# A fused attention and feed-forward kernel: the second-layer block ahead of a new group's first layer, and another priority for the output copies

## Chip, cores and metric

The kernel runs on 1 core of one Trainium2 chip. The metric is the time of the kernel in device microseconds; the median of 3 runs stands for the kernel.

## What is computed

A long-short attention over B=4, H=8, S=768, D=64 gives the tokens of a two-layer feed-forward block with a rational activation. Cut to what matters:

```python
scores_l = scale * (q @ k.T)              # only where |i - j| < 16
scores_s = scale * (q @ k_blockmax.T) + log(32)   # 24 blocks of 32 keys
a = softmax(concat(scores_l, scores_s))
x = a @ concat(v, v_blockmean)            # -> x [3072 tokens, 512]

h = x @ w_in                              # 512 -> 2048
P = a0 + a1*h + a2*h*h + a3*h*h*h
Q = 1 + |b0|*|h| + |b1|*h*h
out = (P / (Q + 1e-6)) @ w_out            # 2048 -> 512
```

## The kernel before

The 3072 tokens are worked in six groups of 512 (`NG`), the 2048 inner columns in 16 chunks of 128 (`NFC`). A step is one chunk of one group, `step = 16 g + fc`; 96 steps make up the feed-forward part. Each step has these parts:

- `moe1` (L390): TensorE (PE) computes the chunk's h into one PSUM bank with twelve 512-column matmuls, eight with xh and four with xl, the upper and lower part of the group's x. `split` (L326) makes these parts at the first chunk of a group, four casts on ScalarE (ACT) and four subtractions on VectorE (DVE).
- `gelu` (L401): the activation. ACT makes the square of h (into tile sq or tq), |h| (ta) and an affine function of h (tu). DVE makes tq for the denominator; ACT takes its reciprocal through a logarithm and an exponential (`ta<-tq`, `ta<-ta`). DVE multiplies tu by h twice (`tu<-tu,h`, then `tu<-tu,cs,h`, the "second product", the last reader of the bank of h), then writes gh, tq and the last tu. GpSimd (POOL) writes gl from tu and ta. gh and gl are the upper and lower part of the activation. In steps without scores sq lies in a PSUM bank, otherwise the square is in tq in SBUF.
- `moe2` (L432): the second-layer block of the chunk three steps back (`LAG`), twelve matmuls into the four banks po_0 to po_3 (gh, gh, gl for each); `second_layer` (L451) takes it from a queue.
- `finish` (L441) at the last chunk of a group: ACT copies po_0 to po_3 into o_0 to o_3, and the DMA queue of SyncE (SP) writes them out. With the lag this falls into the new group's third step (fc = 2); the new group's first second-layer block, one step later, needs the copied banks.

PSUM holds four banks for po, two for h, and two for scores and sq. The attention of a half (64 tokens) is woven into the steps: every fourth step from step 14 on, two steps into each of groups 1 to 4 among them, PE multiplies probabilities and values (`av`, in one of the two banks of h) and makes new scores (`sc`), DVE masks the scores and takes the maxima (`ss`, `sm`), ACT takes the exponentials (`ss<-ss,sm`), and POOL normalizes them. ACT copies av to x (`x<-av`).

The tiles ta, tq and tu have two buffers, so ta of a chunk can be written only when gl of the chunk two steps back has been made; gh and gl have three.

The order of work has two regimes. In the first 14 steps (`NSTRICT`) each engine issues in the order of the text (`Kept`, L78 to L95). Afterwards PE alone is still kept in that order, while the Tile scheduler orders DVE, ACT, POOL and SP by a timeline simulation and by priorities: `tc.high_priority(offset=n)` puts what stands in it n places ahead. `split` has the offset 60 (L557), the activations -15 (L601), the attention 40 (L603). In the main loop (L547 to L625) `moe1` of a step comes first, then the activations, then the attention of the step, and `second_layer` (L623) comes last. At a border between groups PE therefore runs h of chunk 0 of the new group, then the block of chunk 13 of the old one, then h of chunk 1, then the block of chunk 14, and so on.

All engine calls pass the helper at L88, so that the profile gives this line for every instruction; tiles tell them apart.

Of the kernel before, what the change touches and what calls it, by code (L numbers as in the profile page):

```python
# [35 lines left out]
NG = NT // GT  # L36
# [24 lines left out]
def tile_kernel(ctx, tc, qw_in, kraw, kwin, vpad, vred, wio, a, b, cmask, cident, cavg, out):  # L61
# [109 lines left out]
    def value_average(av, vt, i):  # L171
        pe.matmul(av[:NK, :], avg[:, AVGW - NK - 4 * i:AVGW - 4 * i], vt[i], start=(i == 0), stop=(i == len(vt) - 1))
# [15 lines left out]
    def att_load(jj):  # L188
        bi, j = divmod(jj, NJ)
        nc.sync.dma_start(out=qw[jj % 2], in_=qw_in[bi, j])  # L190
        nc.sync.dma_start(out=kw[jj % 2][:, 0:NKC - 1], in_=kwin[bi, j])

    def key_blocks(jj):
        bi, j = divmod(jj, NJ)
        if j < 2 and bi > 0 or jj in (HPG, HPG + 1):
            dve.tensor_copy(kw[jj % 2][:, NKC - 1], ksum[bi])
# [51 lines left out]
    def load_v(jj):  # L248
        bi, j = divmod(jj, NJ)
        vt = vres[jj] if jj < HPG else vw[jj % 2]  # L250
        nc.sync.dma_start(out=vt[0:NKW, :], in_=vpad[bi, j * HQ:j * HQ + NKW, :])
        if j < 2 and bi == 1:
            nc.sync.dma_start(out=vt[NKW:NK, :], in_=vnext)
        elif j < 2 and bi > 1:
            nc.gpsimd.dma_start(
                out=vt[NKW:NK, :].rearrange("n (q d) -> n q d", q=4),
                in_=vsum[bi].rearrange("p c e -> p (c e)"))

    def turned(jj, early=False):
        pt = ps_h.tile([P, 512], F32, tag="h", name=f"pt{jj}") if early else ps_a.tile([P, 512], F32, tag="a", name=f"pt{jj}")  # L260
        for pr in range(NPAIR):
            pe.transpose(out=pt[:NK, pr * P:(pr + 1) * P], in_=att[jj][:, pr, :], identity=ident)
            if pr == NPAIR - 1:
                att[jj] = pt
            yield
# [60 lines left out]
    def split(g):  # L326
        if g == 0:
            return x32[0]
        xh = xp.tile([P, NCC, GT], F32R, tag="xh", name=f"xh{g}")
        xl = xp.tile([P, NCC, GT], F32R, tag="xl", name=f"xl{g}")  # L330
        for c in range(NCC):
            act.copy(xh[:, c], x32[g][:, c])
            dve.tensor_tensor(xl[:, c], x32[g][:, c], xh[:, c], op=ALU.subtract)
        return xh, xl
# [55 lines left out]
    def moe1(g, fc, xh, xl):  # L390
        h = ps_h.tile([P, GT], F32, tag="h", name=f"h{g}_{fc}")
        k = 0
        wt = weights(fc)
        for i, x in ((0, xh), (1, xh), (0, xl)):
            for cc in range(NCC):
                pe.matmul(h, wt[:, i, 0, cc * P:(cc + 1) * P], x[:, cc, :], start=(k == 0), stop=(k == 3 * NCC - 1))
                k += 1
        gh = gp.tile([P, GT], F32R, tag="gh", name=f"gh{g}_{fc}")
        gl = gp.tile([P, GT], F32R, tag="gl", name=f"gl{g}_{fc}")
        return gh, gl, gelu(h, gh, gl, g, fc)  # L400
# [31 lines left out]
    def moe2(fc, po, gh, gl, between):  # L432
        wt = weights(fc)
        for t in range(TPG):
            with tc.high_priority(offset=40):
                lead(between)
            ts_ = slice(t * P, (t + 1) * P)
            for i, (l, r) in enumerate(((gh, 0), (gh, 1), (gl, 0))):
                pe.matmul(po[t], l[:, ts_], wt[:, r, 1, :], start=(fc == 0 and i == 0),
                   stop=(fc == NFC - 1 and i == 2))  # L440

    def finish(g, po):
        for t in range(TPG):
            o = gp.tile([P, DM], F32, tag="o" if g < NG - 1 else "gl" if t % 2 else "gh", name=f"o{g}_{t}", bufs=4 if g < NG - 1 else 3)
            if g == NG - 1 and t % 2:
                dve.tensor_copy(o, po[t])
            else:
                act.copy(o, po[t])
            nc.sync.dma_start(out=out[g * GT + t * P:g * GT + (t + 1) * P, :], in_=o)

    def second_layer(step, queue, po, pt):  # L451
        if step >= LAG:
            g, fc, r = queue.pop(0)
            if fc == 0:
                po = [ps_o.tile([P, DM], F32, tag="o", name=f"po{g}_{t}") for t in range(TPG)]
            moe2(fc, po, *r, pt)
            if fc == NFC - 1:
                finish(g, po)
        return po

    cross = [tc.dram_tile([P, NKB, NPAIR, SQ], F32, name=f"cross{i}") for i in range(4)]
# [31 lines left out]
    def lead(chain, all_of=False):  # L493
        for _ in chain or ():
            if not all_of:
                return
# [5 lines left out]
    def whole(jj):  # L502
        yield from scores(jj)
        yield
        yield from values(jj)
# [42 lines left out]
    queue, po, x, gelus = [], None, None, {}  # L548
    for step in range(NG * NFC + LAG):
        g, fc = divmod(step, NFC)  # L550
        strictly = step < NSTRICT
        if step == NSTRICT:
            strict -= {dve, act, gps}
            for chain in [c for k, c in sorted(chains.items(), key=str)] + [gelus.pop(s) for s in sorted(gelus)]:
                lead(chain, True)
        if g < NG:
            if fc == 0:  # L557
                with tc.high_priority(offset=60):
                    x = split(g)
            gh, gl, gelus[step] = moe1(g, fc, *x)  # L560
            queue.append((g, fc, (gh, gl)))
        for what in STEP.split() if strictly else ():
            kind, n = what[0], int(what[1:] or 0)
            if kind == "g":
                lead(gelus.get(step - n))
            elif kind == "q":
                lead(prods.get(step - n))
            elif kind == "h":
                for jj in halves.get(step - n, ()):
                    lead(chains.setdefault(("h", jj), whole(jj)))  # L570
            elif kind == "k":
                for jj in halves.get(step - n, ()):
                    if jj > HPG + 1:
                        key_blocks(jj)
            elif kind == "l":
                for jj in halves.get(step - n, ()):
                    load_v(jj)
            elif kind == "a":
                for jj in halves.get(step - n, ()):
                    att_load(jj + 2)  # L580
            elif kind == "w" and fc + n < NFC and g == 0:
                lead(chains.setdefault(("w", fc + n), w_split(fc + n)))
            elif kind == "u":
                for f, *args in reduces.get(step, ()):
                    f(*args)
                for f, *args in loads.get(step, ()):
                    f(*args)
            elif kind == "P":
                pt = (z for jj in halves.get(step - n, ()) for z in turned(jj))
                po = second_layer(step, queue, po, pt)  # L590
                lead(pt, True)
            elif kind == "v" and step < LAG:
                if step == 0:
                    vf = ps_o.tile([P, DM], F32, tag="o", name="vf1")
                for i in range(2 * step, 2 * step + 2):
                    value_average(vf, fv1, i)
                if step == LAG - 1:
                    second_means(vf)
        if strictly:
            continue  # L600
        if step in gelus:  # L601
            with tc.high_priority(offset=-15):
                lead(gelus.pop(step), True)  # L603
        with tc.high_priority(offset=40):
            if step - 4 >= NFC - 2 and halves.get(step - 4):
                both_values(halves[step - 4][0])
            for jj in halves.get(step, ()):
                key_blocks(jj)
            if step in halves:
                chain = [scores(jj, sc=sc) for jj, sc in zip(halves[step], both_scores(halves[step][0]))]  # L610
            else:
                chain = ()
            for _ in range(5):
                for c in chain:
                    lead(c)
            for jj in halves.get(step - CROSS, ()):
                if jj >= 2 * HPG:
                    crossed(jj)
            for jj in halves.get(step, ()):
                load_v(jj)  # L620
                if jj + 2 < NHALF:
                    att_load(jj + 2)
        po = second_layer(step, queue, po, None)  # L623
        for f, *args in reduces.get(step, []) + loads.get(step, []):
            f(*args)  # L625

# [55 lines left out]
```

## Time and profile before

| | |
|---|---|
| median of 3 runs | 656.73 us (656.24, 659.31, 656.73) |
| the profiled execution: time | 654.91 us |
| the profiled execution: span | 653.1 us |
| granted TensorE clock, mean | 0.99 |
| DMA | 77.00 MB, mean 118 GB/s |

A row of a timeline or group of the profile names the start and duration in us, the engine, the line, the operation, output tile <- input tiles, shapes and the count; in brackets stand the idle time ahead of the row and what ended it. Rows of several instructions (x8) are back to back. The names of tiles leave out the chunk number there, so that the block is told by its place in time: the borders between groups lie near 155 to 167 us (group 0 to 1), 257 to 267, 357 to 367, 457 to 466 and 554 to 563 us. A matmul of a block counts at the rate of the block, since matmuls overlap in the rows.

### The profile page before, as it was taken

How to read it: one execution, taken by the hardware profiler on the slowest of the kernel's cores; microseconds unless marked ns; L12 is line 12 of the kernel's file. 1: busy time of each engine (PE TensorE's matmuls, PEld its weight loads, DVE VectorE, ACT ScalarE, POOL GpSimd, SP SyncE). 2: the span in 40 equal slices, each digit the busy share in tenths (PEclk: the TensorE clock that was granted, in tenths of full speed). 3: DMA queues.
4: the chain of work that ended last, by engine and by line, in shares of the span. 5: the costliest groups of instructions: out<-in, count | busy, mean ns of one | idle time of the engine just before them, and what ended most of it. 6: DMA issues, size and time to landing. Idle time of an engine off the chain costs nothing.

```text
span 653.1 us, 11832 instructions
## 1 busy us (share of the span) xinstructions
PE 627.3 (96%) x4068; PEld 499.4 (76%) x4068; DVE 577.2 (88%) x1148; ACT 460.4 (70%) x1036; POOL 258.9 (40%) x350
## 2 busy tenths in 40 slices
PE   8897989999999899999999999999999999999997
PEld 5664767776778688788888778888788888888886
DVE  5589999999989999988999989888888888988885
ACT  3979879977677667677677677577687576765652
POOL 1737567744343244343333333433433432222221
PEclk9989889999999999999999999999999999999999
DMA  9997643503354333242343253142152220010001
GB/s 323 333 321 240 239 166 112 182 25 114 107 171 131 102 122 120 84 166 95 112 127 113 73 193 86 63 128 66 64 174 83 64 86 2 13 52 1 0 2 64
DMA packets 51559, 77.00 MB, mean 118 GB/s; under 512 B 6068, under 2 KB 33076, under 8 KB 49580
## 3 DMA queue, kind: packets, MB, share of 16 engines
q1 hardware_dynamic: 50796, 75.80, 35.4%
q8 instruction: 32, 0.52, 0.3%
q10 hardware_dynamic: 576, 0.25, 0.1%
q0 software_dynamic: 128, 0.20, 0.1%
q14 instruction: 27, 0.22, 0.1%
HBM read 61.31 MB, written 14.73 MB: 116 GB/s over the span
## 4 chain that ended last, share of the span: by engine, by line
PE 60%; DVE 19%; ACT 9%; POOL 4%; issue 4%; DMA 2%; SPq 0%; DVEq 0%; POOLq 0%; ACTq 0%
PE po L88 27%; PE h L88 25%; DVE tu L88 6%; DVE tq L88 5%; PE sc L88 3%; POOL ss L88 3%; ACT ss L88 3%; DVE gh L88 3%; PE av L88 3%; ACT ta L88 2%; POOL gl L88 1%; DVE ss L88 1%; PE pt L88 1%; DMA kres<-in_kraw_dram 1%; PE vf L88 1%
## 5 line engine op out<-in xcount | busy, mean ns | idle before, releaser
L88 POOL TENSOR_TENSOR gl<-tu,ta 128x512 fp32r<-128x512 f32 x96 | 129.7, 1351 | 291.1 <-DVE tu L88 169.9
L88 POOL TENSOR_SCALAR ss<-ss,sm 128x120 f32<-128x120 f32 x192 | 98.6, 535 | 89.7 <-DVE sm L88 89.5
L88 PE MATMUL po<-wearly,gh 128*128 128x512 f32 x384 | 125.2, 408 | 1.4 <-ACT o L88 1.2
L88 ACT ACTIVATE ta<-tq,cs 128x512 f32<-128x512 f32 x96 | 69.5, 725 | 74.5 <-DVE tq L88 73.7
L88 PE MATMUL po<-w,gh 128*128 128x512 f32 x384 | 120.3, 394 | 0.0
L88 PE MATMUL h<-xh,wearly 128*128 128x512 f32 x384 | 98.1, 396 | 3.0 <-DVE tu L88 2.3
L88 PE MATMUL h<-xh,w 128*128 128x512 f32 x384 | 95.0, 389 | 0.0
L88 PEld LDWEIGHTS h<-xh,wearly 128*128 128x128 f32 x384 | 71.4, 188 | 23.5 <-DVE tu L88 4.5
L88 PEld LDWEIGHTS po<-wearly,gh 128*128 128x128 f32 x384 | 71.2, 193 | 19.4 <-ACT o L88 3.1
L88 ACT ACTIVATE ss<-ss,sm 128x120 f32<-128x120 f32 x192 | 73.4, 387 | 14.6 <-DVE sm L88 14.4
L88 PEld LDWEIGHTS h<-xh,w 128*128 128x128 f32 x384 | 72.0, 188 | 15.2 <-DVE tu L88 0.2
L88 PEld LDWEIGHTS po<-w,gh 128*128 128x128 f32 x384 | 70.8, 188 | 15.7 <-issue 1.3
L88 DVE SCALAR_TENSOR_TENSOR gh<-tu,cs,ta 128x512 fp32r<-128x512 f32 x96 | 73.8, 769 | 9.5 <-ACT ta L88 1.8
L88 ACT ACTIVATE ta<-h,cs 128x512 f32<-128x512 f32 x96 | 65.5, 682 | 19.1 <-POOL gl L88 18.9
L88 PE MATMUL po<-wearly,gl 128*128 128x512 f32 x192 | 76.3, 398 | 0.0
L88 DVE SCALAR_TENSOR_TENSOR tu<-tu,cs,tq 128x512 f32<-128x512 f32 x96 | 73.3, 763 | 2.5
L88 PE MATMUL po<-w,gl 128*128 128x512 f32 x192 | 74.9, 390 | 0.0
L88 ACT ACTIVATE tu<-h,cs 128x512 f32<-128x512 f32 x96 | 74.8, 779 | 0.0
L88 DVE SCALAR_TENSOR_TENSOR tu<-tu,cs,h 128x512 f32<-128x512 f32 x96 | 71.2, 742 | 2.2
L88 DVE SCALAR_TENSOR_TENSOR tq<-tq,gh 128x512 f32<-128x512 f32 x96 | 68.9, 718 | 2.8
L88 DVE TENSOR_TENSOR tu<-tu,h 128x512 f32<-128x512 f32 x96 | 64.9, 676 | 0.0
L88 DVE SCALAR_TENSOR_TENSOR tq<-tq,cs,ta 128x512 f32<-128x512 f32 x48 | 54.7, 1141 | 9.0 <-ACT ta L88 8.6
(72 smaller groups left out, 928.0 us busy)
## 6 DMA issues: line engine op xcount, KB each, us to landing
wr<-in_wio_dram SPq DMA_DIRECT2D x15, 1024.0 KB
cross<-tb SPq DMA_DIRECT2D x32, 256.0 KB
vw<-in_vpad_dram SPq DMA_DIRECT2D x42, 192.0 KB
kw<-in_kwin_dram SPq DMA_DIRECT2D x40, 192.0 KB
pts<-cross SPq DMA_DIRECT2D x96, 64.0 KB
out_dram<-o SPq DMA_DIRECT2D x24, 256.0 KB
qw<-in_qw_dram SPq DMA_DIRECT2D x40, 128.0 KB
kr<-in_kraw_dram SPq DMA_DIRECT2D x12, 384.0 KB
```

Of the source, the lines that this page charges most:

```text
L88: out = getattr(self.engine, name)(*args, **kw)
```

## The change

At the first chunk of groups 1 to 5 the second-layer block of the old group's chunk 13 is written ahead of `split` and `moe1` of the new group, instead of behind them at the end of the step. And `finish` gets `high_priority(offset=60)`.

```diff
--- before.py
+++ after.py
@@ -455,7 +455,8 @@
                 po = [ps_o.tile([P, DM], F32, tag="o", name=f"po{g}_{t}") for t in range(TPG)]
             moe2(fc, po, *r, pt)
             if fc == NFC - 1:
-                finish(g, po)
+                with tc.high_priority(offset=60):
+                    finish(g, po)
         return po
 
     cross = [tc.dram_tile([P, NKB, NPAIR, SQ], F32, name=f"cross{i}") for i in range(4)]
@@ -553,6 +554,9 @@
             strict -= {dve, act, gps}
             for chain in [c for k, c in sorted(chains.items(), key=str)] + [gelus.pop(s) for s in sorted(gelus)]:
                 lead(chain, True)
+        ahead = fc == 0 < g < NG
+        if ahead:
+            po = second_layer(step, queue, po, None)
         if g < NG:
             if fc == 0:
                 with tc.high_priority(offset=60):
@@ -620,7 +624,8 @@
                 load_v(jj)
                 if jj + 2 < NHALF:
                     att_load(jj + 2)
-        po = second_layer(step, queue, po, None)
+        if not ahead:
+            po = second_layer(step, queue, po, None)
         for f, *args in reduces.get(step, []) + loads.get(step, []):
             f(*args)
```

On PE, the only difference in the whole program is the place of h_0 at the five borders. The rows below are PE's at the border between group 1 and 2, before; h_0 and h_1 are first-layer blocks of the new group, the po block is chunk 13 of the old group.

```order
L88 MATMUL h_0_2943<-xh_2933,wearly 128x512 x8
L88 MATMUL h_0_2943<-xl_2934,wearly 128x512 x4
L88 MATMUL po_0_2108<-w_1505,gh_13_2720 128x512 x2
L88 MATMUL po_0_2108<-w_1505,gl_13_2721 128x512
L88 MATMUL po_1_2109<-w_1505,gh_13_2720 128x512 x2
L88 MATMUL po_1_2109<-w_1505,gl_13_2721 128x512
L88 MATMUL po_2_2110<-w_1505,gh_13_2720 128x512 x2
L88 MATMUL po_2_2110<-w_1505,gl_13_2721 128x512
L88 MATMUL po_3_2111<-w_1505,gh_13_2720 128x512 x2
L88 MATMUL po_3_2111<-w_1505,gl_13_2721 128x512
L88 MATMUL h_1_2986<-xh_2933,wearly 128x512 x8
L88 MATMUL h_1_2986<-xl_2934,wearly 128x512 x4
```

The same place after the change:

```order
L88 MATMUL po_0_2108<-w_1505,gh_13_2720 128x512 x2
L88 MATMUL po_0_2108<-w_1505,gl_13_2721 128x512
L88 MATMUL po_1_2109<-w_1505,gh_13_2720 128x512 x2
L88 MATMUL po_1_2109<-w_1505,gl_13_2721 128x512
L88 MATMUL po_2_2110<-w_1505,gh_13_2720 128x512 x2
L88 MATMUL po_2_2110<-w_1505,gl_13_2721 128x512
L88 MATMUL po_3_2111<-w_1505,gh_13_2720 128x512 x2
L88 MATMUL po_3_2111<-w_1505,gl_13_2721 128x512
L88 MATMUL h_0_2955<-xh_2945,wearly 128x512 x8
L88 MATMUL h_0_2955<-xl_2946,wearly 128x512 x4
L88 MATMUL h_1_2986<-xh_2945,wearly 128x512 x8
L88 MATMUL h_1_2986<-xl_2946,wearly 128x512 x4
```

h_0 now stands behind the twelve matmuls of the block and directly ahead of h_1; the blocks behind h_1 keep their places.

On DVE the scheduler takes the products of chunk 0 later. These rows stand directly behind gh_15, the upper part of the old group's last chunk, at the same border, before:

```order
L88 SCALAR_TENSOR_TENSOR tq_0_2959<-sq_0_2961,cs,ta_0_2958 128x512
L88 SCALAR_TENSOR_TENSOR tq_15_2890<-tq_15_2890,gh_15_2887 128x512
L88 TENSOR_TENSOR tu_0_2960<-tu_0_2960,h_0_2943 128x512
L88 SCALAR_TENSOR_TENSOR tu_15_2891<-tu_15_2891,cs,tq_15_2890 128x512
L88 SCALAR_TENSOR_TENSOR tu_0_2960<-tu_0_2960,cs,h_0_2943 128x512
L88 SCALAR_TENSOR_TENSOR gh_0_2956<-tu_0_2960,cs,ta_0_2958 128x512
L88 SCALAR_TENSOR_TENSOR tq_0_2959<-tq_0_2959,gh_0_2956 128x512
L88 SCALAR_TENSOR_TENSOR tu_0_2960<-tu_0_2960,cs,tq_0_2959 128x512
L88 SCALAR_TENSOR_TENSOR tq_1_3002<-sq_1_3004,cs,ta_1_3001 128x512
L88 TENSOR_TENSOR tu_1_3003<-tu_1_3003,h_1_2986 128x512
L88 SCALAR_TENSOR_TENSOR tu_1_3003<-tu_1_3003,cs,h_1_2986 128x512
L88 SCALAR_TENSOR_TENSOR gh_1_2999<-tu_1_3003,cs,ta_1_3001 128x512
```

And after:

```order
L88 SCALAR_TENSOR_TENSOR tq_15_2890<-tq_15_2890,gh_15_2887 128x512
L88 SCALAR_TENSOR_TENSOR tu_15_2891<-tu_15_2891,cs,tq_15_2890 128x512
L88 SCALAR_TENSOR_TENSOR tq_0_2971<-sq_0_2973,cs,ta_0_2970 128x512
L88 TENSOR_TENSOR tu_0_2972<-tu_0_2972,h_0_2955 128x512
L88 SCALAR_TENSOR_TENSOR tu_0_2972<-tu_0_2972,cs,h_0_2955 128x512
L88 SCALAR_TENSOR_TENSOR tq_1_3002<-sq_1_3004,cs,ta_1_3001 128x512
L88 TENSOR_TENSOR tu_1_3003<-tu_1_3003,h_1_2986 128x512
L88 SCALAR_TENSOR_TENSOR gh_0_2968<-tu_0_2972,cs,ta_0_2970 128x512
L88 SCALAR_TENSOR_TENSOR tu_1_3003<-tu_1_3003,cs,h_1_2986 128x512
L88 SCALAR_TENSOR_TENSOR tq_0_2971<-tq_0_2971,gh_0_2968 128x512
L88 SCALAR_TENSOR_TENSOR gh_1_2999<-tu_1_3003,cs,ta_1_3001 128x512
L88 SCALAR_TENSOR_TENSOR tu_0_2972<-tu_0_2972,cs,tq_0_2971 128x512
```

The rows of chunk 15 step ahead of those of chunk 0; the second product of chunk 1 (`tu_1_3003<-tu_1_3003,cs,h_1_2986`) comes as the ninth row instead of the eleventh, and the last tu of chunk 0 as the twelfth instead of the eighth. Ahead of gh_15 nothing moves at this border. Further on, in the step of the scores, the two products of chunk 2 stand behind the eight score instructions; before they stood ahead of them (at the border between group 2 and 3 one of the two did).

On ACT the copies move among the exponentials. These are its rows at the border between group 2 and 3, two steps into group 3, before; ss are the exponentials of the scores, o the output copies, ta_2 the activation of chunk 2:

```order
L88 COPY x_4162<-av_4163 128x4x128
L88 ACTIVATE ta_2_4147<-tq_2_4148,cs 128x512
L88 ACTIVATE ta_2_4147<-ta_2_4147 128x512
L88 ACTIVATE ss_4199,sm_4200<-ss_4199,sm_4200 128x120 x2
L88 COPY o_0_4251<-po_0_3210 128x512
L88 ACTIVATE ss_4199,sm_4200<-ss_4199,sm_4200 128x120 x2
L88 COPY o_1_4254<-po_1_3211 128x512
L88 ACTIVATE ss_4205,sm_4206<-ss_4205,sm_4206 128x120 x4
L88 COPY o_2_4257<-po_2_3212 128x512
L88 COPY o_3_4260<-po_3_3213 128x512
L88 ACTIVATE sm_4200<-sm_4200 128x4
```

And after:

```order
L88 COPY x_4162<-av_4163 128x4x128
L88 ACTIVATE ta_2_4147<-h_2_4132,cs 128x512
L88 ACTIVATE tu_2_4149<-h_2_4132,cs 128x512
L88 COPY o_0_4251<-po_0_3210 128x512
L88 ACTIVATE ta_2_4147<-tq_2_4148,cs 128x512
L88 ACTIVATE ss_4199,sm_4200<-ss_4199,sm_4200 128x120 x3
L88 COPY o_1_4254<-po_1_3211 128x512
L88 ACTIVATE ss_4199,sm_4200<-ss_4199,sm_4200 128x120
L88 ACTIVATE ss_4205,sm_4206<-ss_4205,sm_4206 128x120
L88 ACTIVATE ta_2_4147<-ta_2_4147 128x512
L88 COPY o_2_4257<-po_2_3212 128x512
L88 ACTIVATE ss_4205,sm_4206<-ss_4205,sm_4206 128x120 x2
```

The next row after this is `COPY o_3_4260<-po_3_3213 128x512`. The first copy moves ahead of ta_2's logarithm, the second exponential of ta_2 moves behind five of the eight ss, the last copy behind seven of them, and the copy of av moves ahead of ta_2's first row. At the borders between groups 1 and 2 and between 3 and 4 the copies keep their place behind ta_2's logarithm; there o_0 stands behind one ss, then come three ss, ta_2's exponential, o_1, three ss, o_2, one ss, and o_3 (before: ta_2's exponential, two ss, o_0, four ss, o_1, two ss, o_2 and o_3). On POOL and SP a few neighbours change places.

## The prediction

> **What bounds the kernel now.** I read the page first, then the waits of TensorE (PE), then the stretches around the five group borders in the timelines of PE, VectorE (DVE), ScalarE (ACT) and GpSimd (POOL). The page gives the busy time of each engine:
>
> ```profile
> PE 627.3 (96%) x4068; PEld 499.4 (76%) x4068; DVE 577.2 (88%) x1148; ACT 460.4 (70%) x1036; POOL 258.9 (40%) x350
> ```
>
> PE is busy for 627.3 of 653.1 us, so all its idle time together is 25.8 us, and no reordering can return more. The waits of PE say how much of that belongs to the borders (us in total, times, longest):
>
> ```profile
> PE av L88 <- DVE tu L88: 4.1, 4, 2.4
> ...
> PE h L88 <- DVE tu L88: 2.3, 4, 0.9
> PE h L88 <- DVE xl L88: 1.6, 2, 1.4
> ...
> PE po L88 <- ACT o L88: 1.2, 2, 1.0
> ```
>
> Steady PE work takes 2.72 us for each block of twelve 512-column matmuls, as the chain of waits shows:
>
> ```profile
> 288.31 2.72 PE po L88 x12
> ```
>
> I call the borders A (group 0 to 1), B, C, D, E, and a block by its chunk: h_0 is the new group's first, po_13 the old group's second-layer block that the change puts ahead of it.
>
> **The change, part one: po_13 ahead of h_0.** PE runs in the order of its list, and only h_0 moves in it; its twelve matmuls end behind po_13 instead of ahead of it, and h_1 follows. What matters is therefore what h_1 waits for. At B and C:
>
> ```profile
> 264.91 0.70 DVE L88 SCALAR_TENSOR_TENSOR tu<-tu,cs,h 128x512 f32<-128x512 f32 x1
> ```
>
> ```profile
> 265.67 2.11 PE L88 MATMUL h<-xh,wearly 128*128 128x512 f32 x8 [0.43 <-DVE tu L88]
> ```
>
> ```profile
> 364.20 2.12 PE L88 MATMUL h<-xh,wearly 128*128 128x512 f32 x8 [0.91 <-DVE tu L88]
> ```
>
> h_1 takes the PSUM bank of h_15, which the second product of chunk 15 frees: it ends at 264.91 + 0.70 = 265.61, and h_1 starts at 265.67. No DVE instruction moves ahead of that product, so h_1 starts then in both versions. Whatever h_0 waited for xl before reappears in the wait of h_1. **Gain at B and C from the order on PE: 0.** At D h_1 waits for nothing, so there is nothing to win. At E the question is whether h_2 now waits for the bank of h_0:
>
> ```profile
> 560.34 0.75 DVE L88 SCALAR_TENSOR_TENSOR tu<-tu,cs,h 128x512 f32<-128x512 f32 x1
> ```
>
> ```profile
> 564.77 1.98 PE L88 MATMUL h<-xh,wearly 128*128 128x512 f32 x8
> ```
>
> The bank is free at 561.09; h_0 comes one block later, 561.09 + 2.72 = 563.81, still 0.96 us ahead of h_2 at 564.77. **E: 0**, and up to +0.3 if the products of h_0, now behind two more of chunk 15, come over 0.96 us later still.
>
> A is the border that can lose. po_13 needs gl_13 at its third matmul:
>
> ```profile
> 158.53 1.27 POOL L88 TENSOR_TENSOR gl<-tu,ta 128x512 fp32r<-128x512 f32 x1
> ```
>
> ```profile
> 160.40 0.50 PE L88 MATMUL h<-xl,wearly 128*128 128x512 f32 x1 [1.44 <-DVE xl L88]
> ...
> 164.24 2.14 PE L88 MATMUL h<-xh,wearly 128*128 128x512 f32 x8 [0.55 <-DVE tu L88]
> ```
>
> gl_13 ends at 159.80. Ten of the twelve matmuls of po_13 follow (10 x 2.72 / 12 = 2.27, to 162.1), then h_0 to 164.8, where before h_1 started at 164.24: +0.6. The wait of h_0 for xl (1.44) disappears, and a wait of po_13 for gl_13 takes its place. I count this 0.6 at nothing, because a later wait of PE for DVE covers it:
>
> ```profile
> 224.53 1.15 PE L88 MATMUL av<-pts,vw 120*64 120x64 f32 x32 [2.40 <-DVE tu L88]
> ```
>
> PE stands 2.40 us there; DVE sets that time, so a PE that is 0.6 later waits 0.6 less. If DVE is itself late by the shift, A costs its +0.6.
>
> **Part two: what moves on DVE at B, C, D.** At the border's step 18 the attention's av matmuls use the PSUM bank of h_1 and wait for its second product:
>
> ```profile
> 274.65 1.15 PE L88 MATMUL av<-pts,vw 120*64 120x64 f32 x32 [0.52 <-DVE tu L88]
> ```
>
> ```profile
> 373.17 1.15 PE L88 MATMUL av<-pts,vw 120*64 120x64 f32 x32 [0.51 <-DVE tu L88]
> ```
>
> ```profile
> 471.98 1.15 PE L88 MATMUL av<-pts,vw 120*64 120x64 f32 x32 [0.69 <-DVE tu L88]
> ```
>
> In the new order that product is the ninth instruction behind gh_15, not the eleventh: two instructions of chunk 0 (about 0.7 us each by the rows below) step behind it, 1.4 us against waits of 0.5 to 0.7. These waits go. But that is no gain by itself: one step on, the new group's second layer reuses the po banks, and waits for the output copies of ACT. Whether PE arrives earlier there matters only if the copies do.
>
> **Part three: the copies, and what stands ahead of them.** Before, at B:
>
> ```profile
> 279.28 0.40 ACT L88 ACTIVATE ss<-ss,sm 128x120 f32<-128x120 f32 x1 [0.19 <-DVE sm L88]
> ...
> 280.05 0.57 ACT L88 COPY o<-po 128x512 f32<-128x512 f32 x1
> 280.52 0.40 ACT L88 ACTIVATE ss<-ss,sm 128x120 f32<-128x120 f32 x1
> ```
>
> ```profile
> 282.31 0.62 PE L88 MATMUL po<-wearly,gh 128*128 128x512 f32 x2
> ...
> 285.40 0.86 PE L88 MATMUL h<-xh,wearly 128*128 128x512 f32 x3
> ```
>
> ACT takes two ss exponentials in 280.05 - 279.28 = 0.77 (0.385 each) and 0.47 for a copy. PE loses 285.40 - 282.31 - 2.72 = 0.37 at B. At C and D:
>
> ```profile
> 379.21 0.38 ACT L88 ACTIVATE ss<-ss,sm 128x120 f32<-128x120 f32 x1
> ```
>
> ```profile
> 380.81 0.63 PE L88 MATMUL po<-wearly,gh 128*128 128x512 f32 x2
> ...
> 383.82 0.73 PE L88 MATMUL po<-wearly,gh 128*128 128x512 f32 x2 [1.04 <-ACT o L88]
> ...
> 385.32 1.98 PE L88 MATMUL h<-xh,wearly 128*128 128x512 f32 x8
> ```
>
> ```profile
> 476.60 0.40 ACT L88 ACTIVATE ss<-ss,sm 128x120 f32<-128x120 f32 x1 [0.19 <-DVE sm L88]
> ```
>
> ```profile
> 479.62 0.62 PE L88 MATMUL po<-wearly,gh 128*128 128x512 f32 x2
> ...
> 482.71 1.98 PE L88 MATMUL h<-xh,wearly 128*128 128x512 f32 x8
> ```
>
> The loss is 1.79 at C and 0.37 at D. The same distance holds at all three: from the first ss to the block h_4 behind the copies it is 6.12, 6.11 and 6.11 us. So the time of h_4 is the start of ss plus the length of ACT's list up to the copies, and I cost both.
>
> The list. Before, ta_2's second exponential stood ahead of the first ss; in the new order it stands among them, and at B and D all eight ss stand ahead of the last copy: 8 x 0.385 + 0.55 (ta_2, below) + 3 x 0.47 + 0.57 = 5.61, then one po block of three matmuls (0.68) and 0.05 for the hand-over: 6.34, **+0.23**. At C seven ss and o_1, o_2 are ahead of o_3: 4.76 + 0.73 = 5.5, **-0.6**.
>
> The start. The scores on DVE (ISA in the order's rows, CUSTOM_DVE in the trace) lose two products that stood ahead of them, but now wait for a chain that had slack: tu_0's last result, gl_0 on POOL, ta_2, tq_2. At B before:
>
> ```profile
> 269.82 1.22 DVE L88 SCALAR_TENSOR_TENSOR gh<-tu,cs,ta 128x512 fp32r<-128x512 f32 x1
> ...
> 271.80 0.75 DVE L88 SCALAR_TENSOR_TENSOR tu<-tu,cs,tq 128x512 f32<-128x512 f32 x1
> ...
> 276.91 0.75 DVE L88 SCALAR_TENSOR_TENSOR tq<-tq,cs,ta 128x512 f32<-128x512 f32 x1
> ...
> 278.96 0.27 DVE L88 CUSTOM_DVE_ANT_0 ss<-sc,mask 128x120 f32<-128x120 f32 x1
> ```
>
> ```profile
> 272.73 1.30 POOL L88 TENSOR_TENSOR gl<-tu,ta 128x512 fp32r<-128x512 f32 x1 [2.23 <-DVE tu L88]
> ```
>
> ```profile
> 278.45 0.63 ACT L88 ACTIVATE ta<-ta 128x512 f32<-128x512 f32 x1
> ```
>
> ```profile
> L88 ACT ACTIVATE ta<-tq,cs 128x512 f32<-128x512 f32 x96 | 69.5, 725 | 74.5 <-DVE tq L88 73.7
> ...
> L88 ACT ACTIVATE ta<-h,cs 128x512 f32<-128x512 f32 x96 | 65.5, 682 | 19.1 <-POOL gl L88 18.9
> ```
>
> tu_0's last result (271.80) goes from eighth to twelfth behind gh_15; four instructions of 0.72 make it 274.68 to 275.43. gl_0 then runs 275.6 to 276.9, ta_2 to 277.6, tq_2 to 278.35, and ta_2's logarithm to 279.07, where ss can start: -0.2 against 279.28. At D I take the same. At C tq_2 stands behind a reduction of another step, which covers this chain, and it was slow:
>
> ```profile
> 376.56 1.32 DVE L88 SCALAR_TENSOR_TENSOR tq<-tq,cs,ta 128x512 f32<-128x512 f32 x1
> ```
>
> It ended at 377.88, and ss started at 379.21 behind both halves of ta_2. The exponential now stands behind ss (-0.55), and with gl_0 out of the way tq_2 may take the 0.75 of B (-0.57): between -0.55 and -1.1, I take -0.9.
>
> One correction is open: DVE beside POOL. gh at 269.82 took 1.22 while gl ran; undisturbed the same instruction takes about 0.75. With gl_15 earlier, the instructions beside it read h or sq from PSUM, and I expect this 0.47 back; but gl_0 now falls beside two DVE instructions of chunk 1 whose inputs all lie in SBUF, which may hold it up by one of them, up to +0.7. Together -0.47 to +0.23; I take -0.1, near the middle, for B and D, and nothing at C, where the reduction covers it. By the Trainium skill, "SBUF — State Buffer", section "Who interferes with whom", a VectorE instruction with two SBUF inputs and a GpSimd one that reads SBUF exclude each other for a whole instruction; by that rule alone gl_0 is held up in full at all three borders, and the estimate would be 656.1 instead of 655.1. That gh took 1.22 agrees with it; gl_0 at 272.73 took an undisturbed 1.30 with DVE at work, which says no more than that DVE then read PSUM.
>
> **The sum.** A 0; B -0.2 - 0.1 + 0.23 = -0.1; C -0.9 - 0.6 = -1.5; D -0.1; E 0. Together -1.7, of the 653.1 us span. The profiled execution took 654.91, 1.8 more than its span; with the change 653.2. The runs of before have a median of 656.73, 1.8 above that execution, and the same difference gives **655.1 us** (656.73 - 1.7, rounded). Bounds: A 0 to +0.6; B and D from -1.0 (PE's own losses there, 0.5 to 0.7 at av and 0.37 at po, all gone) to +0.5; C from -2.3 (0.51 + 1.79 gone) to 0; E 0 to +0.3. All lows together -4.3, all highs +1.9.
>
> **The rivals.**
> 1. *The waits vanish whole (faster).* If ss starts early enough that all copies are done in time, av (0.52 + 0.51 + 0.69) and po (0.37 + 1.79 + 0.37) return 4.25 us: 652.5. If h_1's and h_0's waits went too (2.3 + 1.6 more), 648.6. For it: all these waits stand at borders. Against: DVE sets h_1's start, and ACT's list ahead of the copies gets no shorter at B and D. Chance 0.15, a third of it for the second kind.
> 2. *A new wait (slower).* The strict list on ACT makes the copies wait behind tq_2's chain. Such a wait of ACT for POOL is in the trace already:
>
> ```profile
> 270.53 0.69 ACT L88 ACTIVATE ta<-h,cs 128x512 f32<-128x512 f32 x1 [1.22 <-POOL gl L88]
> ```
>
> If the chain through gl_0 moves ss 1.22 later instead of earlier, B and D cost 1.22 + 0.23 each, C 1.22 - 0.6, A its 0.6: +4.1, 660.8. It decides as soon as ss starts more than 279.28 - 274.65 = 4.63 us behind the start of av. Against: the chain worked out above arrives 0.2 early. Chance 0.08.
> 3. *Nothing.* Copies and DVE cancel at C as well, and the time is that of before: 656.7. For it: the longest term, C, hangs on one reduction whose place is chance. Chance 0.25.
>
> My forecast, a gain at C alone, has 0.52.
>
> **How the numbers follow.** A measurement of this kernel can tell about 0.5%, 3.3 us, from no change. The range runs from 652.4 (the sum with all lows, and rival 1 of the first kind) to 658.6 (all highs); outside lie rival 2, the second kind of rival 1 and a little of the spread of the runs (656.24 to 659.31), 0.18 in all. Faster by more than 0.5% is below 653.4: rival 1 and a small part of the forecast's low side, 0.18. Slower is above 660.0: rival 2, 0.08. The rest, 0.74, is within 0.5%.
>
> **What would show it.** Right: at B and C h_1 still waits for DVE and starts as long after the old group's po_12 as before; av at B, C, D waits for nothing; at C the copies' wait shrinks by about 1.5 us, at B and D the distance from the first ss to h_4 grows to about 6.3; at A po_13 waits for gl_13 and the 2.40 wait shrinks by 0.6. Wrong: if h_1 comes earlier at B or C, if ss starts over 0.5 us from where I put it, or if h_2 waits for the bank of h_0.

## The result, and the profile after

| | before | with the change |
|---|---|---|
| median | 656.24 us (13 runs) | 661.33 us (13 runs) |
| ratio, with 95% interval | | 1.0073 (1.0051 to 1.0095) |
| profiled execution: time, span | 654.91, 653.1 us | 662.64, 660.9 us |
| granted clock of that execution | 0.990 | 0.977 |

The change costs 0.7%, about 5 us. The forecast was 655.1, a small gain. In the page's busy row PE and its weight loads grew most, by 5.3 and 6.7 us, though PE executes the same instructions. The row of the clock shows part of the reason. It gives the granted clock in 40 equal slices of the span, in tenths. The first and the sixth slice are lower than before, and the eleventh, 165 to 182 us, has an 8 (before, all slices from the seventh on were 9):

```profile
PE 632.6 (96%) x4068; PEld 506.1 (77%) x4068; DVE 579.3 (88%) x1148; ACT 459.3 (70%) x1036; POOL 257.4 (39%) x350
...
PEclk8989879999899999999999999999999999999999
```

The row of the clock before:

```profile
PEclk9989889999999999999999999999999999999999
```

The waits of PE after the change, in the same columns as before:

```profile
PE po L88 <- POOL gl L88: 4.1, 1, 4.1
PE po L88 <- ACT o L88: 3.4, 6, 0.8
...
PE av L88 <- DVE tu L88: 3.0, 2, 2.4
...
PE h L88 <- DVE tu L88: 1.0, 1, 1.0
PE av L88 <- DVE xl L88: 0.7, 1, 0.7
```

The waits of h for xl and most of those for tu are gone. Two have come: one of 4.1 us for gl, and six for the output copies in place of two.

To see where the time went, I took the start of each h block from the timelines of both traces and subtracted (after minus before, us; the step's number is 16 g + fc):

```
step 15   +3.39   (the start; the code is the same up to here)
step 18   +6.50   two blocks behind border A
step 26   +5.63
step 27   +7.18
step 34   +5.76   two blocks behind border B
step 36   +6.68   behind B's copies
step 47   +6.66
step 50   +6.65   two blocks behind border C
step 52   +5.62   behind C's copies
step 55   +6.22
step 66   +6.20   two blocks behind border D
step 68   +7.25   behind D's copies
step 95   +7.26
```

The first 3.39 us is no part of the change: the start scatters by that much between executions (the other traces below stand between -0.7 and +3.3 at step 15). What is left up to step 95 is 3.87. It falls at A (+2.24 by step 26), at the attention of step 26 (+1.55), at B ahead of the copies (-1.42, at h_1 and h_2), at the copies of B, C and D (+0.9, -1.0, +1.05), and ahead of step 55 (+0.6). The spans differ by 7.8 us: another half microsecond falls behind the last output copy; the end of the section on the prediction comes back to it.

**Border A.** The timelines of PE and POOL:

```profile
158.54 0.61 PE L88 MATMUL po<-w,gh 128*128 128x512 f32 x2
163.25 0.80 PE L88 MATMUL po<-w,gl 128*128 128x512 f32 x1 [4.09 <-POOL gl L88]
```

```profile
158.65 3.31 POOL L88 TENSOR_SCALAR ss<-ss,sm 128x120 f32<-128x120 f32 x4 [7.29 <-DVE sm L88]
161.93 1.26 POOL L88 TENSOR_TENSOR gl<-tu,ta 128x512 fp32r<-128x512 f32 x1
```

po_13 stops at its third matmul until gl_13 comes, behind four normalizations, at 163.19. Before, h_0 filled that time. And then the clock falls (the last columns are the granted clock, the DMA share and GB/s):

```profile
162.00:164.00 2.00, 0.76 (x2) 0.66 (x3) 2.00 (x3) 0.78 (x2) 2.00 (x3) 0.60 0.23 85
164.00:166.00 2.00, 2.00 (x7) 1.52 (x6) 1.71 (x3) 1.34 (x3) 1.49 (x4) 0.50 0.17 60
166.00:168.00 2.00, 2.00 (x6) 1.61 (x5) 2.00 (x5) 0.59 (x1) 0.00 (x0) 0.50 0.64 210
168.00:170.00 2.00, 2.00 (x7) 1.55 (x7) 1.97 (x3) 0.00 (x0) 1.16 (x1) 0.70 0.18 60
170.00:172.00 2.00, 2.00 (x10) 1.67 (x9) 1.78 (x2) 0.65 (x2) 0.50 (x2) 1.00 0.31 93
```

The clock is at half from about 162.4 to 169.2 us, and PE works in it from 163.25 on: the ten matmuls left of po_13 take 167.68 - 163.25 = 4.43 us, where the steady rate gives 2.27. The Trainium skill has this in "TensorE: Matmul & The Clock Gate", section "Part 1: The HAM clock gate (the "warmup" mystery)": an idle TensorE falls to half its clock, as a free-running window of about 3.4 us decides. The trace agrees in the 0.50, and in the window: by the clock column the half clock lasts (0.40 + 0.50 + 0.50 + 0.30) x 2 / 0.50 = 6.8 us, two times 3.4. Where it differs stands in the last section.

**Borders B and D.** The DVE rows of B ahead of the scores, with POOL's:

```profile
281.33 1.66 DVE L88 SCALAR_TENSOR_TENSOR tu<-tu,cs,tq 128x512 f32<-128x512 f32 x1
283.19 1.81 DVE L88 SCALAR_TENSOR_TENSOR tq<-tq,cs,ta 128x512 f32<-128x512 f32 x1 [0.21 <-ACT ta L88]
284.93 0.27 DVE L88 CUSTOM_DVE_ANT_0 ss<-sc,mask 128x120 f32<-128x120 f32 x1
```

```profile
280.86 1.57 POOL L88 TENSOR_TENSOR gl<-tu,ta 128x512 fp32r<-128x512 f32 x1 [5.90 <-DVE tu L88]
283.15 1.30 POOL L88 TENSOR_TENSOR gl<-tu,ta 128x512 fp32r<-128x512 f32 x1 [0.72 <-ACT ta L88]
```

The first DVE row is the last tu of chunk 1, the second tq of chunk 2; each takes about 0.75 us undisturbed, here 1.66 and 1.81, beside gl_0 and gl_1. At D they are 1.66 and 1.80. At B and D only the second of them reaches ss, because tq_2 has to wait for ta_2, and ta_2 for the end of gl_0:

```profile
282.47 0.69 ACT L88 ACTIVATE ta<-h,cs 128x512 f32<-128x512 f32 x1 [0.61 <-POOL gl L88]
```

The tu is done at 282.99, ta_2 only at 283.16. Then tq_2 takes 1.06 us more than 0.75: gl_1 started 0.04 us ahead of it. So ss comes late on ACT, and h_4 with it:

```profile
285.67 0.38 ACT L88 ACTIVATE ss<-ss,sm 128x120 f32<-128x120 f32 x1
```

```profile
288.80 0.73 PE L88 MATMUL po<-wearly,gh 128*128 128x512 f32 x2 [0.50 <-ACT o L88]
290.42 0.73 PE L88 MATMUL po<-wearly,gh 128*128 128x512 f32 x2 [0.66 <-ACT o L88]
292.08 1.08 PE L88 MATMUL h<-xh,wearly 128*128 128x512 f32 x4
```

From ss to h_4 it is 6.41 us (6.34 in the prediction). But ss is 6.39 us later than before while h of step 34 is 5.76 later: +0.63, where the prediction has -0.3. At D it is the same to 0.1 us:

```profile
483.55 0.38 ACT L88 ACTIVATE ss<-ss,sm 128x120 f32<-128x120 f32 x1
```

```profile
489.96 1.99 PE L88 MATMUL h<-xh,wearly 128*128 128x512 f32 x8
```

6.41 us again, and ss +0.75 against step 66. At C the list is shorter (5.56 us; 5.5 in the prediction), and the step gains:

```profile
385.38 0.38 ACT L88 ACTIVATE ss<-ss,sm 128x120 f32<-128x120 f32 x1
```

```profile
390.94 1.30 PE L88 MATMUL h<-xh,wearly 128*128 128x512 f32 x5
```

### The profile page after: what moved, and what is told of

It is laid out like the page before. It is cut to its first block, busy times and chain, and to the rows that moved or that the text cites. A ratio compares the mean times of both kernels' runs of the same rounds, so it can differ in the third digit from the quotient of the medians.

```text
span 660.9 us, 11836 instructions
## 1 busy us (share of the span) xinstructions
PE 632.6 (96%) x4068; PEld 506.1 (77%) x4068; DVE 579.3 (88%) x1148; ACT 459.3 (70%) x1036; POOL 257.4 (39%) x350
## 4 chain that ended last, share of the span: by engine, by line
PE 60%; DVE 19%; ACT 8%; DMA 5%; issue 4%; POOL 3%; DVEq 0%; SPq 0%; POOLq 0%; ACTq 0%
PE po L88 28%; PE h L88 26%; DVE tu L88 6%; DVE tq L88 5%; PE av L88 3%; DVE gh L88 3%; ACT ss L88 2%; PE sc L88 2%; ACT ta L88 2%; POOL ss L88 2%; DMA vr<-in_vpad_dram 2%; DMA kw<-in_kwin_dram 1%; POOL gl L88 1%; DMA vf<-in_vpad_dram 1%; DVE ss L88 1%
## 5 line engine op out<-in xcount | busy, mean ns | idle before, releaser
L88 DVE SCALAR_TENSOR_TENSOR tu<-tu,cs,tq 128x512 f32<-128x512 f32 x96 | 76.9, 801 | 2.4
```

The source lines that it names most:

```text
L88: out = getattr(self.engine, name)(*args, **kw)
```

## The experiments

The theories: (1) the stall at A, above all through the clock; (2) the copies at B and D, because DVE and POOL hold each other up; (3) the start alone. The ratio of each run is to the kernel before, with its 95% interval. The edits are shown against the kernel with the change, if nothing else is said; "..." marks what is left out. "Shift" is the start of an h block against the trace of before, as in the table above.

**The change without A.**

```diff
-        ahead = fc == 0 < g < NG
+        ahead = fc == 0 and 1 < g < NG
```

> The change at borders B to E alone; at A the order of before. Theory 1 (the cost is at A: the second-layer block of chunk 13 stands 4.1 us waiting for gl, and the granted clock then is 0.5 for about 7 us): no such wait, the clock at 155 to 170 us stays 1.00, and the time is that of before within +-0.3%, ratio 0.998 to 1.003. Theory 2 (the cost is at the copies of B and D, first ss late because DVE and POOL hold each other up): ratio 1.004 to 1.008, as for the whole change. Theory 3 (the cost is the start, ahead of step 14, where the profile of the change was already 3.4 us late): the ratio scatters with the start and says nothing of the borders.

Measured: 659.82 us, 1.0053 (1.0030 to 1.0077). The clock from 140 to 180 us stays 1.00, and the shift is +1.25 at step 15 and +1.22 at step 26: A costs nothing. Over B's copies (step 34 to 36) the shift goes from +1.36 to +2.28, over C's (50 to 52) from +2.29 to +1.23, over D's (66 to 68) from +1.79 to +2.84, as in the whole change. The ratio is where theory 2 has it: most of the cost is not at A.

**A alone, without the priority.**

```diff
-                with tc.high_priority(offset=60):
-                    finish(g, po)
+                finish(g, po)
...
-        ahead = fc == 0 < g < NG
+        ahead = fc == 0 and g == 1
```

> The reorder at border A alone, without the priority. Theory 1: the 4.1 us wait for gl and the dip of the clock are there, h two steps behind the border is about 3 us later than before, and 2 to 4 us of it are left at the end: ratio 1.003 to 1.006. Theory 2: ratio 0.999 to 1.002, since the later waits of PE for DVE (0.43 at B, 0.91 at C) take the delay back. Theory 3: as theory 2.

Measured: 657.85 us, 1.0029 (1.0004 to 1.0053). The wait for gl is 4.1 us again; the shift goes from +1.10 at step 15 to +3.69 at step 18 and +2.84 at step 26. So A costs as well, and the two parts, 0.29% and 0.53%, add up to the 0.73% of the change within their intervals. The trace shows too what becomes of A's delay. The wait of av for DVE, which the prediction had as its cover, has not shrunk:

```profile
227.35 1.97 PE L88 MATMUL av<-pts,vw 120*64 120x64 f32 x32 [2.40 <-DVE tu L88]
```

It was 2.40 before, too. DVE waited for the late h blocks too: between 160 and 180 us it was busy 19.71 us before and is busy 18.26 here (third figure behind the comma; the trace of before first, then this one).

```profile
160.00:180.00 20.00, 18.97 (x135) 14.85 (x136) 19.71 (x43) 13.51 (x28) 7.46 (x10) 1.00 0.36 113
```

```profile
160.00:180.00 20.00, 19.04 (x128) 15.42 (x129) 18.26 (x27) 10.61 (x18) 7.50 (x10) 0.86 0.22 71
```

At B, where this kernel has the old order, the shift falls from +4.29 at step 31 to +2.86 at step 34. In the run without A, with the new order there, it falls by the same 1.43, from +2.79 to +1.36. There a late PE gets time back, in either order, because DVE frees the bank of h_15 at its own time. What is paid back so is the clock dip at step 26, not A's delay: the unchanged wait of 2.40 us says that up to there DVE is as late as PE. In all five traces of this document with such a dip the shift falls by 1.43 from step 31 to 34; in the four others that have a wait at step 26, it moves by 0.06 at most.

**The priority alone.** Against the kernel before.

```diff
             if fc == NFC - 1:
-                finish(g, po)
+                with tc.high_priority(offset=60):
+                    finish(g, po)
```

> The priority of the output copies alone, no reorder. All theories: PE, DVE and ACT have the rows of before, so ratio 0.999 to 1.001; what it scatters is the spread of the start. If the priority itself were the cause: 1.004 or more.

Measured: 656.70 us, 1.0009 (0.9987 to 1.0032): nothing. The shift is +2.70 at step 15 and +2.64 at step 95, so the start is all that differs.

**The reorder alone, without the priority.**

```diff
-                with tc.high_priority(offset=60):
-                    finish(g, po)
+                finish(g, po)
```

> The reorder at all five borders without the priority. Theory 1 and 2: ratio 1.005 to 1.009, as the whole change or a little worse, since the last copies stand behind all eight ss. If the priority were the cause: 0.998 to 1.002.

Measured: 660.48 us, 1.0063 (1.0040 to 1.0086). The reorder is the cause. At D the shift rises more than in the whole change, from +2.95 at step 67 to +6.59 at step 69, since all eight ss now stand ahead of o_2; the times of the two kernels don't tell them apart.

**A alone, with twelve matmuls without use ahead of po_13.** They go into the bank of h_0, which h_0 then overwrites; the priority of `split` goes from 60 to 72 with them. The edits of the run with A alone are left out here.

```diff
+        filled = None
         if ahead:
+            filled = ps_h.tile([P, GT], F32, tag="h", name=f"h{g}_{fc}")
+            for k in range(12):
+                pe.matmul(filled, weights(fc)[:, 0, 0, :P], weights(fc)[:, 1, 0, :], start=True, stop=True)
             po = second_layer(step, queue, po, None)
...
-                with tc.high_priority(offset=60):
+                with tc.high_priority(offset=60 if filled is None else 72):
                     x = split(g)
-            gh, gl, gelus[step] = moe1(g, fc, *x)
+            gh, gl, gelus[step] = moe1(g, fc, *x, filled)
```

> The reorder at A alone, with twelve matmuls without use (2.72 us, into the bank of h_0, which h_0 then overwrites) ahead of the second-layer block, so that TensorE stands 4.1 - 2.7 = 1.4 us instead of 4.1. Up to there nothing else moves; behind step 18 some DVE and ACT rows of groups 1 and 2 do. Theory 1a (the length of the stall brings the clock down, and that is most of the loss at A): the granted clock between 160 and 172 us stays 1.00, h of step 18 starts +0.3 to +0.8 us later than before instead of +2.5 (relative to step 15). Rival 1b (the loss is the wait for gl itself, whatever PE does meanwhile): +2.3 or more, as without the filling. Time: 1a ratio 0.999 to 1.003; 1b 1.002 to 1.005.

Measured, the place that the run was made for:

```profile
161.50 0.50 PE L88 MATMUL po<-w,gl 128*128 128x512 f32 x1 [1.40 <-POOL gl L88]
```

```profile
160.00:164.00 4.00, 2.60 (x12) 2.06 (x12) 3.47 (x5) 1.89 (x3) 3.74 (x7) 1.00 0.18 66
164.00:168.00 4.00, 4.00 (x20) 3.30 (x18) 3.97 (x7) 1.40 (x3) 0.91 (x1) 1.00 0.40 131
```

The clock stays at 1.00, and the shift goes from +1.61 at step 15 to +2.07 at step 18: +0.46, against +2.59 without the filling, though gl comes no earlier and PE does 2.7 us more. So the clock is 2.1 of the 2.6 us. The total, 659.10 us, 1.0046 (1.0022 to 1.0070), misses the expectation: the filling makes the scheduler place DVE and ACT rows of step 18 and later differently, and the shift jumps from +2.36 to +5.28 at step 20, part of which comes back at step 27 (+1.91). The total therefore says nothing about A.

**A alone, with gl_13 on DVE.** The edits of the run with A alone are left out again.

```diff
-        gps.tensor_tensor(gl, tu, ta, op=ALU.mult)
+        (dve if g * NFC + fc == NSTRICT - 1 else gps).tensor_tensor(gl, tu, ta, op=ALU.mult)
```

> The reorder at A alone, with gl of chunk 13 made by DVE instead of POOL, which has four normalizations ahead of it. The wait of the second-layer block for gl gets shorter by about 2 us, to about 2; DVE's later rows come 0.7 us later. Theory 1a: no dip or a short one, h of step 18 +0.5 to +1.0 relative to step 15, ratio 0.999 to 1.003. Rival 1b: +0.5 to +1.0 as well; what tells them apart is whether the clock falls. If neither holds and POOL is not the cause: +2.3 or more.

Measured: 656.09 us, 1.0009 (0.9987 to 1.0031).

```profile
157.07 0.50 PE L88 MATMUL po<-w,gl 128*128 128x512 f32 x1 [2.04 <-DVE gl L88]
```

```profile
156.00:158.00 2.00, 0.93 (x3) 0.79 (x4) 1.79 (x4) 2.00 (x5) 2.00 (x3) 0.87 0.00 0
158.00:160.00 2.00, 2.00 (x6) 1.51 (x6) 1.69 (x3) 0.42 (x1) 2.00 (x5) 0.50 0.06 23
160.00:162.00 2.00, 2.00 (x9) 1.60 (x8) 2.00 (x4) 0.90 (x2) 0.67 (x2) 0.78 0.29 109
```

The clock fell here too, but after a wait of 2.04 us and for half the time, some 3.4 us, and the shift is -0.73 at step 15 and -0.70 at step 18. h_1 follows h_0 at once and comes 0.28 us late (-0.45 at step 17); the 0.55 us that it waited for DVE before took up the rest, and ahead of h_2, where PE stood before as well, nearly all of the 0.28 is made good. So it is POOL's place for gl_13 that made A cost anything.

**B to E, with gl_0 of groups 2 to 4 on DVE.**

```diff
-        ahead = fc == 0 < g < NG
+        ahead = fc == 0 and 1 < g < NG
...
-        gps.tensor_tensor(gl, tu, ta, op=ALU.mult)
+        (dve if fc == 0 and 1 < g < NG - 1 else gps).tensor_tensor(gl, tu, ta, op=ALU.mult)
```

> The change at B to E (as in the run without A), with gl of chunk 0 of groups 2 to 4 made by DVE instead of POOL. Theory 2a (DVE and POOL hold each other up: tu_1 took 1.66 and tq_2 1.81 instead of 0.75 beside gl_0 and gl_1): these two take 0.75 to 1.2, ss starts 0.5 to 1.3 us earlier at B and D, and B and D together cost 0.5 us or less instead of 2; ratio 1.001 to 1.004 against 1.0053 without. Rival 2b (the later place of chunk 0 in DVE's order is the cost, not the beside): DVE is 0.7 us later by the added instruction, ss starts as late as or later than in the change, and the ratio is 1.005 to 1.007.

Measured: 655.47 us, 0.9978 (0.9957 to 1.0000), against 1.0053 with gl_0 on POOL. The same DVE rows of B:

```profile
277.26 0.69 DVE L88 TENSOR_TENSOR gl<-tu,ta 128x512 fp32r<-128x512 f32 x1
277.86 0.75 DVE L88 SCALAR_TENSOR_TENSOR tu<-tu,cs,tq 128x512 f32<-128x512 f32 x1
278.70 0.75 DVE L88 SCALAR_TENSOR_TENSOR tq<-tq,cs,ta 128x512 f32<-128x512 f32 x1
```

```profile
280.12 0.38 ACT L88 ACTIVATE ss<-ss,sm 128x120 f32<-128x120 f32 x1
```

DVE has an instruction more and is done sooner: 1.66 and 1.81 are now 0.75 and 0.75. ss is 0.84 later than before where h of step 34 is 1.50 later: -0.66 instead of +0.63. Of these 1.29 us, 0.24 come from the earlier end of gl_0, which lets ta_2 and tq_2 start earlier, and 1.05 from tq_2 itself. Now tq_2 starts ahead of gl_1, by 0.08 us, and it is gl_1 that is held up:

```profile
278.78 1.83 POOL L88 TENSOR_TENSOR gl<-tu,ta 128x512 fp32r<-128x512 f32 x1 [7.78 <-ACT ta L88]
```

The kernel before had the same pair in the same order: tq_2 at 276.91 took 0.75, and gl_1 1.66:

```profile
277.16 1.66 POOL L88 TENSOR_TENSOR gl<-tu,ta 128x512 fp32r<-128x512 f32 x1 [3.14 <-DVE tu L88]
```

From step 31 to 37 the shift falls by 0.45, from 63 to 69 by 0.57, where in the run without A it rose by 1.03 in the latter. Theory 2a holds, rival 2b falls.

**gl_0 on DVE alone, in the order of before.** The same edit to gl, in the kernel before.

> The kernel before, its order and priorities unchanged, with gl of chunk 0 of groups 2 to 4 made by DVE. Theory 2a (POOL and DVE hold each other up only in the new order, where gl_0 stands beside DVE rows that read SBUF alone): nothing to win here, since gl_0 ran beside rows that read PSUM; DVE has one instruction of 0.7 us more at three borders: ratio 0.999 to 1.003. Rival 2c (gl_0 on DVE is a gain in itself, and the reorder had no part in the 0.9978 of the run with both): 0.996 to 0.999.

Measured: 657.21 us, 1.0012 (0.9986 to 1.0037). No gain shows: gl_0 on POOL costs time only where the reorder puts it. This trace has its clock dip at step 26, which stands in the order of before: a wait of 2.44 us, the clock at 0.50 from about 228 to 234, and the shift goes from +3.32 to +6.20 at step 27. So the +1.55 that the trace of the change shows there isn't the change's either; it comes and goes with the execution.

**The whole change, gl_0 and gl_13 on DVE.** Both edits to gl together.

> The whole change, with gl of chunk 0 of groups 2 to 4 and gl of chunk 13 at border A made by DVE: both suspected costs taken out. Theories 1 and 2a together: A costs nothing at the steps behind it (the wait for gl is about 2 us, hidden by DVE's own delay of h_1), B to D gain about 1.4 us as before: ratio 0.996 to 1.000. If a third cost is at work in the change: 1.002 or more.

Measured: 655.34 us, 0.9988 (0.9970 to 1.0006). The shift is +1.33 at step 15, +1.38 at step 18, +1.33 at step 31, +0.90 at step 37, +0.58 at step 55, +0.02 at step 95: A costs nothing, and B, C and D gain 0.44, 0.32 and 0.57. With the two costs out, no loss of the change is left. That it or the run before it beats the kernel before by more than a measurement tells isn't shown: both intervals reach 1.0.

## Why the prediction was wrong, point by point

- **h_1 starts with DVE at B and C, so the order on PE wins nothing there.** Right. Where PE came late it lost its wait at B and got 1.43 us back, with the old order as with the new. At E nothing moved, as predicted.
- **A: "+0.6 ... I count this 0.6 at nothing".** Wrong twice. With the clock at 1.00 the term was good (+0.46 with the filling). But the wait it rests on is 4.09 us long, and the trace shows PE at half its clock for some 6 us behind it: +2.6 to +3.1 at step 18. The working had the granted clock at full throughout. And the cover failed: the 2.40 us wait for DVE stayed at 2.44, because h_0 and h_1 came late to DVE as well. A wait of PE for DVE covers a late PE only if DVE isn't late by the same cause; the condition stood in the prediction and was taken the wrong way.
- **av's waits at B, C, D go.** Right, except that this is no gain by itself, as the prediction says.
- **The length of ACT's list: 6.34 and 5.5.** Right: 6.41, 5.56 and 6.41.
- **The start of ss at B and D: "-0.47 to +0.23; I take -0.1".** This step failed. DVE beside POOL cost not one collision but two: gl_0 held the last tu of chunk 1 (+0.9), and gl_1, which follows that tu at once, held tq_2 (+1.06). The working saw only gl_0. Up to tq_2 its chain was good: less the shift of 5.76, gl_0 ended at 276.67 at B (276.9 in the working) and ta_2 at 277.40 (277.6), because the held tu was done by then. The step that failed is "tq_2 to 278.35": tq_2 took 1.81 instead of 0.75 and ended at 279.24. So ss is 0.93 (B) and 1.05 us (D) later than forecast, and each costs about 1 us instead of winning 0.1. The rule of the Trainium skill cited there, "SBUF — State Buffer", section "Who interferes with whom", is what the traces show: DVE's 1.66 and 1.81 beside POOL's gl, 0.75 without. Its estimate in the prediction, 656.1, counted one collision as well.
- **C: -1.5.** Half right: -1.0 behind the copies. The list gained its 0.6, but ss came 0.5 us earlier, not 0.9: the held tu took 1.66 us here too, with DVE busy from it through the reduction and tq_2 to the scores, so the reduction did not cover it as the working had it:

```profile
381.05 1.66 DVE L88 SCALAR_TENSOR_TENSOR tu<-tu,cs,tq 128x512 f32<-128x512 f32 x1
382.63 1.21 DVE L88 TENSOR_REDUCE vs<-vr 96x32 f32<-96x1024 f32 x1
383.76 0.96 DVE L88 SCALAR_TENSOR_TENSOR tq<-tq,cs,ta 128x512 f32<-128x512 f32 x1
384.64 0.27 DVE L88 CUSTOM_DVE_ANT_0 ss<-sc,mask 128x120 f32<-128x120 f32 x1
```

  And 0.6 is lost again at step 55, where av waits 0.54 us for DVE. Before, it did not wait there:

```profile
405.25 1.15 PE L88 MATMUL av<-pts,vw 120*64 120x64 f32 x32 [0.54 <-DVE tu L88]
```

- **The rivals.** The second, a new wait on ACT behind tq_2's chain, is what happened at B and D, at 1.0 us each instead of 1.45, with A's delay beside it. Its own sign was there: at B ss starts 285.67 - 279.82 = 5.85 us behind the start of av, more than 4.63. It had a chance of 0.08. I had weighed it by a wait for gl_0's end alone. At C it is not what happened; C still gained.

What stays open: the trace of the run without A loses 1.6 us between steps 15 and 95. Its dip of the clock at step 26, which isn't the change's, cost 1.57 and gave 1.43 back at B, so about 1.5 us are left for B to D. Its median is 3.5 us above that of before, and the runs of that kernel go from 657.1 to 663.5 us. Two things on record fill part of the gap. From the end of the last output copy to the end of the span it takes 3.80 us, against 2.98 before; in the traces of all four kernels that have both the reorder at B to E and the priority it is 3.54 to 3.80, in the others 2.98 to 3.18. Why is not shown. And the mean granted clock of its runs has a median of 0.984, against 0.987 for the runs of before next to them: 0.003 x 656 us / 0.50 = 4 us more at half clock, which is worth up to 2 us of PE work. More short waits of PE, each of which may bring the clock down in some executions, would do that; which ones, a single profile of each kernel can't show, and I didn't try it apart.

## What to carry to other kernels

Before a block is moved ahead, look up what its operands wait for: the block that stood in its place may have been the work that hid that wait. A stall of TensorE isn't only its own length; price the clock behind it. And when an order on one engine changes, check which instructions of DVE and POOL now lie beside each other, and follow a late one to the next.

## What the runs showed of the hardware that was not expected

- The granted clock fell to 0.50 after waits of PE shorter than the 3.4 us window of the Trainium skill: after 2.04 us (gl_13 on DVE), and after 2.40 to 2.44 us at step 26 in five of the ten traces that have this wait, while it stayed at 1.00 in the other five, the trace of before among them. After 1.40 us (the filling) and 1.44 us (h_0's wait for xl before) it stayed. It was then at half for 3.4 us or for 6.8 us: 6.8 behind the 4.09 us of A, 3.4 behind the 2.04.
- An instruction of DVE with both inputs in SBUF that took 0.75 us alone took up to 1.81 beside POOL's gl. The one that started later was held up, by however little it was later: tq_2 took 1.81 when it started 0.04 us behind gl_1, and 0.75 when it started 0.08 ahead of it, where gl_1 took 1.83 instead of 1.3. Giving DVE the 0.69 us of gl_0 to do brought ss 1.29 us earlier than leaving it to POOL.
